# Attention with a soft mixture of experts on one core: contiguous tables and loads, one more weight quarter held early, plain maxima for the last queries

## The chip, the cores and the metric

The kernel runs on one core of one Trainium2 chip. The metric is the device time of one execution in microseconds (us); lower is better. The kernel before has a median of 422.11 us over three runs (420.61 to 422.81).

## What is computed

Causal attention with a cumulative bias over 8 batches of 8 heads (576 positions, 64 channels), then a mixture of experts in which softmax weights over all 4608 tokens mix the tokens into 32 slots, eight two-layer networks work on the slots, and a second softmax spreads the slots back.

```python
scores = scale * q @ k.T                       # per head, 576 x 576
bias   = -(cum[:, None] - cum[None, :])        # cum = cumsum(max(s, 0))
scores = where(causal, -1e9, scores + min(bias, 0))
attn   = exp(scores - scores.max(-1)); attn /= attn.sum(-1) + 1e-9
x      = attn @ v                              # then tokens x 512
logits = x @ phi                               # 32 slots, 4 for each expert
d = softmax over tokens(logits); slot_in = d.T @ x
slot_out[e] = max(slot_in[e] @ w1[e], 0) @ w2[e]
out = softmax over slots(logits) @ slot_out
```

## The kernel before, in words

The work goes by 32 pairs p of heads, four to a batch. A table written out by hand, ORDER, sets the order of every step; each step issues its instructions on its engines as the table comes to it, and each engine then works through its own list in that order. `x.p` below is step x of pair p.

**Scores.** `load` fetches a pair's transposed queries and keys. `cast` (ScalarE) rounds them into a tile `w` and `low` (VectorE) writes the remainders behind, so that three passes of matmuls give nearly full precision. A tile `g` holds in a few rows the cumulated bias and, later, the row maxima, each as a high and a low part; the matmuls of `mx` and `s` take `g` as one more factor. `mx.p.i` (TensorE, L367) computes approximate scores, `red.p.i.a` (VectorE, L379) takes their maxima for head a: a custom instruction adds a mask of 0 and -3e38 and reduces, and each is followed by one that reads its accumulator. Group 0 are keys 0 to 287 of the last 128 queries, group 1 the remaining 288 keys of these queries, started from group 0's maximum. `f0`, `f1`, `f2` split and transpose the maxima, and `md` sends them into `g` (two DMAs); `cum` sends the bias rows (two DMAs).

**Attention.** `s` (L429) computes exact transposed scores less the maxima, `ex` (ScalarE, L440) the exponentials, `cut` (GpSimd, L447) the causal corner, `zc` and `z` the sums over key blocks, `load_v` fetches the values (two DMAs), `ax` and `a` (L511, L522) multiply with them, and `sm` (L551) adds up the denominators of a batch in one bank.

**Normalization.** After a batch's last `sm`, `e1` takes the reciprocals (L631, L632) and `rw` writes them to a table `rs` in DRAM (L636). `rd.p` reads a pair's rows of the table back, spread to 64 partitions per head (L561, two DMAs), `nr.p` (VectorE, L584) multiplies. `nat` transposes for TensorE's next product and `lt` forms the logits. The last two pairs take `rb` (L572), which spreads by matmuls instead of through DRAM.

**The expert stage.** The weights are 64 quarters of 512 KB each. 23 are fetched into `pre` during the attention (`pre.i`), 27 into space that falls free at its end (`get.i`), and the rest by `refill` into quarters that have been used. The weight and output DMAs are all issued by SyncE (SP) in program order. `mlp1` (L983) and `mlp2` (L1011) are the two layers for four experts at a time; `ct`, `cd` and `ct7` transpose the second softmax's weights of batches; `pick` (L1020) selects each slot's own expert out of the products; `two` (L1040) and `heads` spread the slots, evict and send out.

```python
1011  nc.tensor.matmul(ps[32 * g:32 * g + 32, :], ht[eg][:, fc, 32 * g:32 * g + 32], ...)
1014  (nc.scalar.copy if eg else nc.vector.tensor_copy)(sos[half][:, eg, :], ps)
```

SP takes its list in order too: an `rd` that waits for its `rw` to land holds back the loads behind it.

## Time and profile before

| | |
|---|---|
| median of three runs | 422.11 us |
| span of the profiled execution | 419.0 us |
| what lies around the span, at the median | 3.1 us |
| TensorE busy | 397.0 us (95%) |
| VectorE, GpSimd, ScalarE busy | 286.6, 281.4, 240.9 us |
| moved by DMA | 82.72 MB in 54037 packets |

The profiled execution's own time is its span of 419.0 us; no other time of that one execution is among those shown. Busy time counts overlapping instructions of an engine once. TensorE runs at full granted clock until its work ends.

### The profile page before, as it was taken

The numbers are of one execution on the slowest core, as the hardware profiler recorded it, in microseconds if no ns is written. First come the engines' busy times: TensorE is split into PE (matmuls) and PEld (weight loads), VectorE is DVE, ScalarE is ACT, GpSimd is POOL, SyncE is SP. The second block draws the span as 40 slices with busy tenths as digits, with TensorE's granted clock in tenths as the row PEclk, the third lists the DMA queues.
The fourth block names the chain that finished last, engine by engine and source line by source line (L and its number), as shares of the span: only waits on it lengthen the run. The fifth ranks groups of instructions, "written<-read, shape, count | busy, mean of one in ns | idle before, by whom it ended". The sixth has DMA issues, their size and how long they took to land.

```text
span 419.0 us, 14779 instructions
## 1 busy us (share of the span) xinstructions
PE 397.0 (95%) x5703; PEld 296.6 (71%) x5703; DVE 286.6 (68%) x1012; ACT 240.9 (58%) x719; POOL 281.4 (67%) x387
## 2 busy tenths in 40 slices
PE   8999999889999999999999999999999999999960
PEld 8877777776777777777777777778777767435540
DVE  7966787987787788777867877787778446211460
ACT  3166666665657666766686768676855753220450
POOL 8178999877877888898878898887888730000000
PEclk9999999999999999999999999999999999999995
DMA  3424578624774558455754674363227869999998
GB/s 128 144 61 145 169 262 227 184 83 143 188 208 140 173 164 236 119 167 161 209 163 144 175 215 140 92 176 115 89 85 179 256 192 390 407 406 408 324 338 294
DMA packets 54037, 82.72 MB, mean 197 GB/s; under 512 B 5584, under 2 KB 40912, under 8 KB 53968
## 3 DMA queue, kind: packets, MB, share of 16 engines
q1 hardware_dynamic: 53952, 81.78, 62.1%
q8 instruction: 45, 0.74, 0.7%
q14 instruction: 24, 0.20, 0.2%
q10 hardware_dynamic: 16, 0.01, 0.0%
HBM read 71.38 MB, written 10.03 MB: 194 GB/s over the span
## 4 chain that ended last, share of the span: by engine, by line
PE 77%; DVE 5%; DMA 5%; issue 2%; POOL 1%; SPq 1%; ACT 1%; DVEq 0%
PE s L429 23%; PE y L522 18%; PE mx L367 10%; PE sum L551 4%; DMA arena<-rs 3%; PE m L1011 3%; PE nat L592 3%; PE m L983 3%; PE lt L655 2%; DVE arena L584 2%; PE sl L776 1%; PE mt L398 1%; DVE junk L379 1%; PE po L1046 1%; PE x L511 1%
## 5 line engine op out<-in xcount | busy, mean ns | idle before, releaser
L379 DVE CUSTOM_DVE_ANT_0 junk<-mx,arena 128x320 bf16<-128x320 f32 (+3 forms) x320 | 125.7, 427 | 51.9 <-PE mx L367 24.7
L440 ACT ACTIVATE arena<-s 128x288 f32<-128x288 f32 (+4 forms) x384 | 115.0, 408 | 30.5 <-PE s L429 29.4
L429 PE MATMUL s<-w 64*128 64x288 f32 (+4 forms) x1152 | 109.2, 304 | 0.2 <-DVE nmin L733 0.2
L522 PE MATMUL y<-arena 128*64 128x512 f32 (+4 forms) x640 | 91.1, 427 | 0.4 <-POOL arena L447 0.4
L429 PEld LDWEIGHTS s<-w 64*128 64x128 f32 (+1 forms) x1152 | 81.8, 177 | 10.2 <-ACT arena L440 1.1
L447 POOL TENSOR_SCALAR_AFFINE_SELECT arena<-arena 128x256 f32<-128x256 f32 (+1 forms) x160 | 67.6, 437 | 21.3 <-ACT arena L440 19.2
L522 PEld LDWEIGHTS y<-arena 128*64 128x64 f32 x640 | 42.9, 137 | 45.1 <-issue 34.1
L468 POOL TENSOR_TENSOR arena<-arena 128x896 f32<-128x896 f32 x31 | 68.2, 2202 | 7.4 <-PE mt L398 4.6
L367 PE MATMUL mx<-w 64*128 64x288 f32 (+4 forms) x384 | 57.2, 302 | 1.5 <-DVE mx L379 0.8
L429 PE MATMUL s<-g 64*128 64x288 f32 (+4 forms) x384 | 56.3, 290 | 0.0
L367 PE MATMUL mx<-g,ones 64*128 64x288 f32 (+4 forms) x384 | 53.5, 300 | 0.0
L339 DVE TENSOR_TENSOR w<-arena,w 128x576 fp32r<-128x576 f32 x64 | 51.2, 820 | 0.1
L470 POOL TENSOR_TENSOR arena<-arena 128x640 f32<-128x640 f32 x31 | 48.0, 1547 | 2.4
L334 ACT CAST w<-arena 128x576 fp32r<-128x576 f32 x64 | 40.3, 677 | 13.4 <-DMA arena<-in_qk_dram 12.6
L534 ACT COPY arena<-y 128x512 f32<-128x512 f32 x32 | 18.8, 588 | 49.5 <-PE y L522 49.5
L367 PEld LDWEIGHTS mx<-w 64*128 64x128 f32 x384 | 39.0, 185 | 4.1 <-DVE mx L379 1.4
L367 PEld LDWEIGHTS mx<-g,ones 64*128 64x128 f32 x384 | 38.6, 185 | 0.3
L429 PEld LDWEIGHTS s<-g 64*128 64x128 f32 (+1 forms) x384 | 35.0, 177 | 0.5
L472 POOL TENSOR_TENSOR arena<-arena 128x384 f32<-128x384 f32 x31 | 31.9, 1029 | 2.4
L584 DVE TENSOR_TENSOR arena<-arena 128x576 f32<-128x576 f32 x30 | 27.7, 929 | 7.3 <-DMA arena<-rs 5.2
L379 DVE CUSTOM_DVE_ANT_0 junk<-mx,arena,mx 128x288 bf16<-128x288 f32 x64 | 30.7, 516 | 2.5 <-PE mx L367 1.2
L379 DVE DVE_READ_ACCUMULATOR2_ANT mx<- 128x1 f32 (+1 forms) x384 | 31.5, 82 | 0.0
(170 smaller groups left out, 515.2 us busy)
## 6 DMA issues: line engine op xcount, KB each, us to landing
arena<-in_qk_dram SPq DMA_DIRECT2D x32, 576.0 KB
pre<-in_w_dram SPq DMA_DIRECT2D x36, 512.0 KB
arena<-in_w_dram SPq DMA_DIRECT2D x19, 512.0 KB
arena<-rs SPq DMA_DIRECT2D x60, 144.0 KB
arena<-in_v_dram SPq DMA_DIRECT2D x32, 256.0 KB
out_dram<-pre SPq DMA_DIRECT2D x16, 256.0 KB
ww<-in_w_dram SPq DMA_DIRECT2D x6, 512.0 KB
out_dram<-arena SPq DMA_DIRECT2D x10, 256.0 KB
```

Source lines behind the costliest of these rows:

```text
L334: nc.scalar.copy(w[:, QO + S * i:QO + S * (i + 1)], st["raw", p][:, i, :])
L339: nc.vector.tensor_tensor(w[:, QO + S * (2 + i):QO + S * (3 + i)], st["raw", p][:, i, :], w[:, QO + S * i:QO + S * (i + 1)].bitcast(F32), ...
L367: nc.tensor.matmul(ps[a][:, d:d + hi - lo], l[r], t[r, KO + lo:KO + hi], start=t is w, stop=t is gt)
L379: nc.vector.tensor_tensor_reduce(out=junk[r, 0:w], in0=ps[r, d:d + w], in1=mask[r, o:o + w], scale=1.0, scalar=m[:, a, 4:5] if i == 1 else ...
L429: nc.tensor.matmul(ps[a][0:n, d:d + hi - lo], t[r, ko + 128 * j:ko + 128 * j + n], t[r, qo + lo:qo + hi], start=x == 0, stop=x == 3)
L440: nc.scalar.activation(st["p", p][0:n, a, o + lo:o + hi], ps[0:n, d:d + hi - lo], AF.Exp, bias=0.0, scale=0.125)
L447: nc.gpsimd.affine_select(d, d, pattern=[[0, 2], [1, n]], compare_op=ALU.is_ge, fill=0.0, base=0, channel_multiplier=-1)
L468: eng.tensor_tensor(z[:, :, 128:576], pt[:, :, 128:576], pt[:, :, 576:1024], op=ALU.add)
L470: eng.tensor_tensor(z[:, :, 256:576], z[:, :, 256:576], pt[:, :, 1024:1344], op=ALU.add)
L472: eng.tensor_tensor(z[:, :, 384:576], z[:, :, 384:576], pt[:, :, 1344:1536], op=ALU.add)
L522: nc.tensor.matmul(y[r, lo - 64:512], vt[:, j, r], st["p", p][:, g, OFF[j] + lo - 128 * j:OFF[j] + 576 - 128 * j], start=(j == 0), stop=(j ...
L584: nc.vector.tensor_tensor(u, u, st.pop(("r", p)), op=ALU.mult)
```

## The change

The scores and the order of the steps stay as they are; ORDER gains one word, `pre.23`. What is changed:

- **A 24th quarter** of weights is fetched during the attention, so that 13 are left to `refill` and not 14. The room comes from smaller tiles: the mask in 16 bits, `w` without its pad, and one buffer fewer for the discarded output `junk` and for `hl`.
- **Group 0** of the maxima is a plain reduce without mask.
- **Rows of `g`** lie on partitions 0, 32, 64 and 96 (bias) and the partition behind each (maxima), so that `md` (from pair 1) and `cum` (from pair 4) are one DMA each.
- **Values** are laid out on the host as the tile wants them, zeros included: one DMA of 2560 bytes a partition.
- **The table `rs`** holds each head's 576 reciprocals in order: `rw` scatters them with two DMAs, and `rd` reads one run of 2304 bytes for each partition and not two of 1152.
- **At the start** fewer memsets on GpSimd.
- **In the expert stage** the eviction of `mlp2` masks and adds the two groups of experts on VectorE, so that `pick` is one matmul. The transposes for `dn` (`cd`) move behind the first half's output, and `ct7` becomes a `ct` ahead of the output of batches 4 and 5.

```diff
-NPRE = 23
+NPRE = 24
...
-    size = dict(raw=2 * S, p=3200, u=S, v=640, z=2 * S, r=S, x=NCH * DM, mask=S - 128, phi=HP * NS, ls=192)
+    size = dict(raw=2 * S, p=3200, u=S, v=640, z=2 * S, r=S, x=NCH * DM, mask=S // 2 - 64, junk=S // 2 - 64, phi=HP * NS, ls=192)
...
-    mask = reg("mask", 0)
+    mask = reg("mask", 0).bitcast(BF16)
...
-        nc.gpsimd.memset(t[:, 0:KO].bitcast(F32), 0.0)
-        for a in (0, 64):
-            nc.gpsimd.memset(t[a:a + 4, 0:KO].bitcast(F32), 1.0)
+        nc.gpsimd.tensor_copy(t[:, 0:KO], ones2[:, 0:1].bitcast(F32).broadcast_to([128, KO]))
...
+    def every32(t, i):
+        return t.bitcast(F32).rearrange("(a r) x -> a r x", r=32)[:, i, :]
...
+            if p >= HP:
+                nc.sync.dma_start(out=every32(gt, 0)[:, KO:KO + S], in_=cumd[2 * p:2 * p + 2])
+                return
...
+                if i == 0:
+                    nc.vector.tensor_reduce(m[:, a, c:c + 1], ps[:, d:d + w], axis=AX.X, op=ALU.max)
+                    continue
...
+            if p:
+                nc.sync.dma_start(out=every32(gt, 1)[:, 0:KO].rearrange("l (c q) -> l c q", c=NCH), in_=hl.bitcast(F32))
+                return
...
-            nc.sync.dma_start(out=vt[:, 0:4, :],
-                              in_=v[b * S:b * S + 512, 128 * hp:128 * hp + 128]
-                              .rearrange("(j p) c -> p j c", p=128))
-            nc.sync.dma_start(out=vt[0:64, 4, :],
-                              in_=v[b * S + 512:b * S + 576, 128 * hp:128 * hp + 128])
+            nc.sync.dma_start(out=reg("v", p % NV), in_=v[p])
...
-            d = st["rs", b, gi].rearrange("(g f a i) x -> g a f (i x)", g=2, f=2, i=4)
             for g in range(2):
-                nc.sync.dma_start(out=r[64 * g:64 * g + 64].rearrange("p (f x) -> p f x", f=2),
-                                  in_=d[g, hp:hp + 1].broadcast_to([64, 2, S // 2]))
+                nc.sync.dma_start(out=r[64 * g:64 * g + 64], in_=st["rs", b, gi][g, hp:hp + 1].broadcast_to([64, S]))
...
-            d = pd.tile([128, SQ], F32, tag="rs", name=f"rs{b}_{gi}")
-            nc.sync.dma_start(out=d, in_=st["sr", b, gi])
+            d = pd.tile([2, 8, S], F32, tag="rs", name=f"rs{b}_{gi}")
+            for g in range(2):
+                nc.sync.dma_start(out=d[g].rearrange("a (i f x) -> f (a i) x", i=4, f=2),
+                                  in_=st["sr", b, gi][64 * g:64 * g + 64])
...
-        (nc.scalar.copy if eg else nc.vector.tensor_copy)(sos[half][:, eg, :], ps)
+        m = again[left[0]][:, DM + 128 + eg:DM + 129 + eg]
+        if eg == 0:
+            nc.vector.tensor_scalar(sos[half], ps, m, None, op0=ALU.mult)
+        else:
+            nc.vector.scalar_tensor_tensor(sos[half], ps, m, sos[half], op0=ALU.mult, op1=ALU.add)
...
-        for eg in range(2):
-            nc.tensor.matmul(ps[:, 0:HC], sel[eg], sos[half][:, eg, :], start=(eg == 0), stop=(eg == 1))
+        nc.tensor.matmul(ps[:, 0:HC], sel, sos[half], start=True, stop=True)
...
-        if cc == 0:
-            ct7()
...
+        if b == 4:
+            ct(B - 1, B)
...
+    cd(4, B)
```

**SP around batch 1's table.** Rows of SP's list from `rw` of batch 1 to the next weight quarter; `rs` is the table, `sr` the reciprocals, `g` the tile of bias and maxima, `hl` the maxima, `cumd` the bias in DRAM. Before:

```order
L636 DMA rs_0_2010<-sr_0_2002 128x72
L411 DMA g_97<-hl_2025 2x5x128 x2
L349 DMA g_96<-cumd 2x576 x2
L561 DMA arena<-rs_0_2010 64x2x288 x4
L491 DMA arena<-in_v_dram 128x4x128
L494 DMA arena<-in_v_dram 64x128
L850 DMA pre<-in_w_dram 128x1024
```

Now:

```order
L646 DMA rs_0_1905<-sr_0_1898 2x32x72 x2
L424 DMA g_97<-hl_1921 4x5x128
L357 DMA g_96<-cumd 4x576
L571 DMA arena<-rs_0_1905 64x576 x4
L506 DMA arena<-in_v_dram 128x640
L860 DMA pre<-in_w_dram 128x1024
```

Twelve DMAs with one `rw` became ten with two; the transfer of the values is one, and the table's writes lead with a dimension of 2.

**TensorE in `mlp1` of the second group of experts.** `m` are the products, `sit` the slots, `ht` the transposed hidden layer. Before:

```order
L983 MATMUL m_7228<-pre,sit 32x512 x4
L983 MATMUL m_7229<-pre,sit 32x512 x4
L1070 MATMUL ct_7241<-ident,e_nat 128x128
L1071 MATMUL cs_7172<-ident,e_nat 32x64
L983 MATMUL m_7228<-pre,sit 32x512 x4
L983 MATMUL m_7229<-pre,sit 32x512 x4
L1000 MATMUL ht_7254<-ident,ww_6568 128x128 x4
```

Now:

```order
L995 MATMUL m_6905<-pre,sit 32x512 x4
L995 MATMUL m_6906<-pre,sit 32x512 x4
L995 MATMUL m_6905<-pre,sit 32x512 x4
L995 MATMUL m_6906<-pre,sit 32x512 x4
L1012 MATMUL ht_6925<-ident,ww_6254 128x128 x4
L1012 MATMUL ht_6931<-ident,ww_6254 128x128 x4
```

The two transposes of batch 7 have left this place.

**TensorE at `pick` of the first half.** `sel` is the selection, `po` the output's product. Before:

```order
L1011 MATMUL m_7364<-pre,wg_6557 32x256 x2
L1020 MATMUL sel_7369<-pre 128x256 x2
L1011 MATMUL m_7364<-arena,wg_6557 32x256 x2
L1011 MATMUL m_7364<-pre,wg_6557 32x256 x2
L1046 MATMUL po<-pre,e_nat 128x256 x8
```

Now:

```order
L1023 MATMUL m_7035<-pre,arena 32x256
L1035 MATMUL sel_7040<-pre 128x256
L1023 MATMUL m_7035<-arena 32x256 x3
L1023 MATMUL m_7035<-pre,arena 32x256
L1061 MATMUL po<-pre,e_nat 128x256 x8
```

Ahead of the first output one selecting matmul stands where two stood.

## Rows read from the trace of the kernel before

**Rows 1.** The page: span, and busy time of each engine.

```profile
span 419.0 us, 14779 instructions
PE 397.0 (95%) x5703; PEld 296.6 (71%) x5703; DVE 286.6 (68%) x1012; ACT 240.9 (58%) x719; POOL 281.4 (67%) x387
```

**Rows 2.** Stages: length; busy PE, PEld, DVE, ACT, POOL; PE clock, DMA share, GB/s.

```profile
117.40:158.50 41.10, 41.10 (x621) 31.73 (x621) 31.46 (x120) 27.55 (x86) 33.48 (x44) 1.00 0.58 168
76.00:117.40 41.40, 37.42 (x569) 28.98 (x569) 34.52 (x112) 28.01 (x86) 32.86 (x44) 1.00 0.54 158
341.00:388.00 47.00, 46.39 (x623) 25.70 (x623) 16.55 (x41) 11.72 (x33) 1.65 (x5) 1.00 1.01 388
388.00:417.50 29.50, 16.40 (x232) 10.31 (x224) 11.21 (x19) 9.93 (x20) 0.00 (x0) 0.86 0.96 333
```

**Rows 3.** The chain that ended last, near 340 us: start, length, work.

```profile
341.08 6.01 DMA arena<-rs
...
347.18 0.76 DVE arena L584
...
348.77 1.22 PE rb L572 x32
```

**Rows 4.** VectorE's instructions by form, 158.5 to 281.8 us: busy, mean ns, idle before.

```profile
L379 DVE CUSTOM_DVE_ANT_0 junk<-mx,arena 128x288 bf16<-128x288 f32 x24 | 10.1, 446 | 9.9 <-POOL arena L447 9.4 <-PE mx L367 0.5
...
L697 DVE TENSOR_REDUCE mt<-ln 128x5 f32<-128x160 f32 x3 | 1.0, 327 | 0.4
```

**Rows 5.** The end in order of time, TensorE: start, length, instruction, idle before.

```profile
360.32 0.41 PE L940 MATMUL cs<-ident,e_nat 64*32 64x64 f32 x6
...
367.55 1.90 PE L983 MATMUL m<-pre,sit 128*32 128x512 f32 x16
369.38 0.33 PE L1070 MATMUL ct<-ident,e_nat 128*128 128x128 f32 x1
...
369.87 1.92 PE L983 MATMUL m<-pre,sit 128*32 128x512 f32 x16
...
384.82 1.13 PE L1020 MATMUL sel<-pre 128*128 128x256 f32 x4
```

**Rows 6.** The same stretch on ScalarE and SP.

```profile
384.52 0.37 ACT L1014 COPY pre<-m 128x256 f32<-128x256 f32 x1 [7.41 <-PE m L1011]
...
388.41 11.69 SPq L1052 DMA_DIRECT2D out_dram<-pre  x16
```

**Rows 7.** SP's issues around batch 1's table, in order of time.

```profile
104.13 0.33 SPq L636 DMA_DIRECT2D rs<-sr  x1
104.77 1.31 SPq L411 DMA_DIRECT2D g<-hl  x2
...
107.03 1.99 SPq L561 DMA_DIRECT2D arena<-rs  x3
```

**Rows 8.** Who waited for that table: VectorE, then TensorE, then pair 8 in batch 2.

```profile
112.91 0.89 DVE L584 TENSOR_TENSOR arena<-arena 128x576 f32<-128x576 f32 x1 [1.60 <-DMA arena<-rs]
...
117.39 0.66 PE L592 MATMUL nat<-ident,arena 128*128 128x128 f32 x4 [0.62 <-DVE mx L379]
...
153.70 0.76 DVE L584 TENSOR_TENSOR arena<-arena 128x576 f32<-128x576 f32 x1
...
155.74 0.49 PE L592 MATMUL nat<-ident,arena 128*128 128x128 f32 x3
```

**Rows 9.** Three short stretches, columns as in group 2.

```profile
21.50:22.00 0.50, 0.50 (x12) 0.50 (x10) 0.50 (x2) 0.01 (x1) 0.00 (x0) 1.00 0.89 184
106.50:108.50 2.00, 2.00 (x14) 0.77 (x12) 1.94 (x11) 0.67 (x2) 1.84 (x3) 1.00 0.03 9
108.50:109.00 0.50, 0.50 (x8) 0.35 (x6) 0.44 (x4) 0.00 (x0) 0.50 (x1) 1.00 0.85 122
```

**Rows 10.** The last pair's values: TensorE waiting, and SP's first issue of them.

```profile
343.46 0.34 PE L511 MATMUL x<-arena 128*64 128x64 f32 x4 [0.46 <-DMA arena<-in_v_dram]
...
338.65 0.55 SPq L491 DMA_DIRECT2D arena<-in_v_dram  x1
```

More of the change, by code (lines that the diff above doesn't have):

```diff
@@ L160 @@
[L160 to L163 removed]
+a.22.0 cut.23.3 red.25.2.0 z.23.1 a.22.1 red.25.2.1 a.22.2 a.22.3 z.23.2 red.25.1.0 a.22.4 ax.23 red.25.1.1 pre.23
+ev.22 load_v.24 s.24.0 low.26.0 z.23.3 evx.23 s.24.2 low.26.1 ex.24.0.0 f0.25 ex.24.0.1 s.24.1 ex.24.2.0 load.28
@@ L288, in tile_attn_softmoe @@
     nc.gpsimd.memset(reg("x", 0)[64:128, 0:DM], 0.0)
-    for i in range(NV):
-        nc.gpsimd.memset(reg("v", i)[64:128, 512:640], 0.0)
     for i in range(NPB):
@@ L1038, in banks, with part @@
         return [bank("po") for _ in range(n)]
-    def two(b, half):
+    def part(b, n, half):
         c = slice(HC * half, HC * half + HC)
-        po = [x.rearrange("p (b c) -> p b c", b=2) for x in banks(4)]
-        for i in range(2):
+        po = [x[:, 0:HC * n].rearrange("p (b c) -> p b c", b=n) for x in banks(4)]
+        for i in range(n):
             for x, r in zip(po, rows):
@@ L1065, in heads @@
                 nc.sync.dma_start(out=outb[b:b + 2, 0:64].rearrange("i t c -> t i c"), in_=ot[:, x, :])
-    def ct7():
-        pa = bank("ct2")
-        nc.tensor.transpose(pa[:, 0:128], et[:, B - 1, 0:128], ident)
-        nc.tensor.matmul(st["cs", 1][rows[3], 1:128:2], et[0:64, B - 1, 128:160], ident[0:64, 0:64], start=True, stop=True)
-        nc.scalar.copy(et[:, B - 1, 0:128], pa[:, 0:128])
-        cd(1, slice(64, 128))
     late_banks = False
     so = again[left[0]][:, 0:DM]
-    sel = [again[left[0]][:, DM + 128 * eg:DM + 128 * eg + 128] for eg in range(2)]
-    ct(1, 4, B - 1)
+    sel = again[left[0]][:, DM:DM + 128]
+    ct(4, B - 1)
     m = mlp1(0)
@@ L1095, in tile_attn_softmoe @@
     stage = [again[i] for i in left[late:]] + [w2q[e, i] for i in range(2) for e in range(NE)]
-    sos = [again[left[1]][:, DM * half:DM * half + DM].rearrange("p (e c) -> p e c", e=2) for half in range(2)]
+    sos = [again[left[1]][:, HC * half:HC * half + HC] for half in range(2)]
     m = chain(mlp2(0, 0), mlp2(0, 1))
@@ L1105, in tile_attn_softmoe @@
     for b in range(0, B, 2):
+        if b == 4:
+            ct(B - 1, B)
         if b == B - 2:
             steps(m)
-        two(b, 0)
+        part(b, 2, 0)
         steps(m, 4)
@@ L1111, in tile_attn_softmoe @@
     late_banks = True
-    two(0, 1)
+    cd(4, B)
+    part(0, 2, 1)
     heads()
     for b in range(2, B, 2):
-        two(b, 1)
+        part(b, 2, 1)
 def constants():
```

175 lines of the change are left out of this document (92 added, 83 removed).

## The prediction

> **What bounds the kernel now.** I read the page first: TensorE is busy for 397.0 of 419.0 us [rows 1]. The stages say where it isn't. From 117.4 to 158.5 us it is busy for all of 41.10 us while VectorE works 31.46, GpSimd 33.48 and the DMA engines 0.58 of the time [rows 2]; the chain of waits there is TensorE's alone up to some 341 us. A shorter instruction on another engine buys nothing in that stretch. Three places are left. Between 76 and 117.4 us TensorE stands still for 41.40 - 37.42 = 3.98 us [rows 2]. Around 341 to 349 us the chain leaves TensorE for the read of the last batch's table, 6.01 us, then VectorE, then `rb` [rows 3]. From there TensorE's list sets when the first output leaves, at 388.41 us [rows 6], and up to then DMA is full as well, share 1.01 at 388 GB/s; behind it the outputs keep DMA at 0.96 and 333 GB/s to the end [rows 2]. A microsecond off the end counts only if the weights and TensorE's list both become shorter before 388.41.
>
> The sum is made against the profiled execution, span 419.0 us; the median of the runs shown is 3.1 us more, and I add that.
>
> **Part by part.**
>
> *The end, 360 to 388 us.* Six `cs` instructions ahead of `mlp1` go; they last 0.41 us [rows 5], and with the overlap of what follows on TensorE I take 0.34. `ct7` goes from the middle: a step of 16 products starts at 367.55 and the next at 369.87, 2.32 us later; the step's own 1.90 leaves 0.42, and from `ct`'s start at 369.38 to 369.87 are 0.49 [rows 5]. I take 0.50, since a step that is followed by its like overlaps it. `pick`'s four instructions last 1.13 [rows 5], so half of them 0.56; against that the first of the old two started without the second group's eviction, 384.82 beside a copy that ends at 384.52 + 0.37 = 384.89 [rows 5, 6]. Now the one must wait for an eviction on VectorE, some 0.25 later, which leaves 0.30. Together 0.34 + 0.50 + 0.30 = 1.14, say 1.15 us. The cover: one quarter of 512 KB less in the queue is 0.524 MB / 388 GB/s = 1.35 us [rows 2], a little more than 1.15, so the weights are out of the way as early as the first output comes. The 24th quarter moves into a stretch where DMA is idle for four tenths of the time, at nothing. The moved `ct` and `cd` fall between 388 and 400 us, where DMA bounds; nothing, or up to 0.4 if they hold up an output. **Term: -1.15**, between 0 (outputs start no earlier) and -1.35.
>
> *The table `rs`, 66 to 117 us.* Batch 1: `rw` is issued at 104.13, the reads begin at 107.03 [rows 7], VectorE waits 1.60 us for them until 112.91, and TensorE later 0.62 for the maxima queued behind that multiplication [rows 8]. What is new has no row. A read of one head was 128 pieces of 1152 bytes and is 64 of 2304. In the half microsecond in which such reads move, 122 GB/s at share 0.85 [rows 9] is 9.0 GB/s for an engine, 128 ns a piece, 1.02 us a transfer over 16 engines; pieces of 512 bytes beside it run at 184 GB/s and 0.89, 40 ns each. If a read's piece keeps its 9.0 GB/s, 2304 bytes cost 256 ns and nothing is gained; if it costs what it did, 128 ns, half: 0.51 us on each of the four transfers of `rd.4` and `rd.5`, 2.0 us. I take the middle, 1.0. SP issues one `md` where two took 1.31 [rows 7], but a second `rw`, 0.33. The writes keep their 288-byte pieces, 8 an engine if 16 engines serve them as now: no cost beyond the second issue. So the table's readers come about 1.0 us earlier, in batch 0 as in batch 1, and of the 3.98 us of standstill I give back a quarter. **Term: -1.0**, between -4.0 (no standstill left) and +2.0 (the rivals). Batches 2 to 6 have nothing to gain: pair 8's multiplication runs at 153.70 to 154.46 and its transposes at 155.74, 1.28 us of slack [rows 8].
>
> *How many engines write the table.* While only transfers that lead with a dimension of 2 are on their way (`md`, `cum`), DMA's share is 0.03 at 9 GB/s [rows 9], half an engine of 16: such transfers are not spread. The Trainium skill, "DMA: Bandwidth & Descriptors", section "Why a DMA increments its semaphore by 16 and not by 1", says that a transfer uses the largest number of engines up to 16 that divides the outermost sizes of both sides, the lowest-numbered ones. By that the new `rw`, which leads with 2, runs on two engines, both halves on the same two; the trace agrees for `md` and `cum`, and no row shows it for a table. The time by it is the first rival's.
>
> *The last pair, 338 to 349 us.* `load_v.31` begins at 338.65 and TensorE waits 0.46 us for it at 343.46 [rows 10]. One DMA in larger pieces, issued without its second half, takes that wait away; the next to be late is `rd.28`, whose landing at about 347.1 holds `rb` at 348.77 [rows 3] and which moves up behind it. **Term: -0.35**, between -0.6 and +1.5 (the table late).
>
> *The rest, at nothing.* Plain maxima: the masked form of 288 keys takes 446 ns, a reduce of 160 elements out of PSUM 327 [rows 4]; at 1 ns more for each of 128 elements it is 455, and the accumulator's read lay beside the next instruction. 64 instructions by -0.08 to +0.05 us are -5 to +3 us of VectorE time, but VectorE idles 9.6 of 41.1 us [rows 2]: covered, and if that cover fails it is in the range of the second term. The mask in 16 bits changes no element count. The memsets on GpSimd lie before the three places named, and I give their shortening nothing. `md` and `cum` as one DMA each save SP issues, and SP's waits are for data.
>
> **Sum:** -1.15 - 1.0 - 0.35 = -2.5. Span 416.5; with 3.1 around it **419.6 us**.
>
> **The rivals.**
>
> *Two engines write the table, at the cheaper price.* 64 pieces an engine instead of 8, at 40 ns: 2.56 - 0.32, the table lands 2.2 us later, the reads give 1.0 back. Batch 1's standstill grows by some 1.2, batch 0 stays (in SP's list a load of values stands ahead of its first read), batches 2 to 6 use up their 1.28 us of slack, the last pair loses 0.6 and its 0.35. Sum -1.15 + 1.2 + 0.6 = +0.65: **422.8 us**, no change. For: the small share of narrow transfers. Against: eight pieces and their latency took under 2.9 us in all [rows 7], so a piece may cost less. Chance 0.24.
>
> *The same at a dearer price; slower.* At 72 ns, the middle in ratio between 40 and 128, the table lands 4.0 us late, 3.0 after the faster reads. SP stands at the first read of each batch, with loads and `md` behind it; TensorE loses 3.0 - 1.28 = 1.7 in each of five batches, 3.0 in batch 1, 1.5 in batch 0 and 2.0 at the last pair: 15.0 - 1.15 = +13.9, **436 us**. It decides once batches 2 to 6 lose too, from a lateness of about 2.5 us, that is from 44 ns a piece. Against: write pieces elsewhere run at 40. Chance 0.12.
>
> *All standstill goes.* The table lands before VectorE asks, and the maxima behind are never late: -4.0 - 1.15 - 0.6, **416.4 us**. For: 1.60 of waiting starts a chain of lateness. Against: VectorE's own multiplications stretched there too, which nothing here mends. Chance 0.15.
>
> *The end does not move*, because outputs queue behind weights or the moved transposes hold them up, and the rest gives 0.5: **421.6 us**. Chance 0.09.
>
> **How the numbers follow.** The forecast has 0.40; its own range is 418.0 to 421.0. Faster or slower by over 0.5%, about what a measurement can tell from no change here, means under 420.0 or over 424.2. Faster: 0.30 of the forecast's 0.40, 0.15 from the third rival, 0.03 from the first: 0.48. Slower: 0.12 of the second and 0.03 of the first's upper part: 0.15. Same: 0.37. The range leaves out the second rival and the lower edge of the third: 415.9 to 424.3.
>
> **What would show it.** Right: first output at about 385 us of the span, TensorE's idle between 76 and 117 us near 3 us, no wait for values at the last pair, no gap between steps at `ct7`'s old place. Wrong: over 4 us between `rw`'s issue and the first read, waits of VectorE for the table in batches 2 to 6, or TensorE idle in a stage that has none now.

## The result, and the profile after

The changed kernel takes 415.56 us (median of 4 runs, 414.87 to 416.38) where the kernel before takes 422.18 (4 runs, 420.61 to 422.81): a ratio of 0.985, 95% interval 0.981 to 0.989, so 6.6 us or 1.6% faster. The forecast was 419.6; the measured time lies 0.3 us below its range. It is closest to the rival "all standstill goes" (416.4), in number only: that rival gave the whole gain of its stretch to a table that lands earlier, and the runs below show another cause.

The page of the changed kernel, to be held against [rows 1]:

```profile
span 413.9 us, 14533 instructions
PE 395.3 (96%) x5699; PEld 295.3 (71%) x5699; DVE 284.0 (69%) x952; ACT 239.6 (58%) x717; POOL 274.8 (66%) x376
```

TensorE works 1.7 us less and the span is 5.1 us shorter, so most of the gain is standstill that is gone. The stretch for which the forecast's largest term was written, and the one that follows it, columns as in [rows 2]:

```profile
76.00:117.40 41.40, 40.76 (x606) 31.23 (x606) 33.26 (x120) 28.89 (x87) 35.70 (x47) 1.00 0.58 182
117.40:158.50 41.10, 40.91 (x620) 31.26 (x616) 31.64 (x113) 28.04 (x86) 34.35 (x45) 1.00 0.56 174
```

Between 76 and 117.4 us TensorE stands still for 0.64 us, against 3.98 before [rows 2]. A stretch fixed in time does not hold the same work in both kernels, so I set a marker into each pair of heads: the 32 products that sum its probabilities, which stand once per pair in TensorE's list. Their starts in both timelines:

| marker | before, us | after, us | ahead by | gained since the marker above |
|---|---|---|---|---|
| sum of pair 5 | 77.50 | 77.32 | 0.18 | |
| pair 6 | 91.57 | 89.97 | 1.60 | 1.42 |
| pair 7 | 102.45 | 99.64 | 2.81 | 1.21 |
| pair 9 | 125.14 | 120.95 | 4.19 | 1.38 |
| pair 12 | 154.98 | 150.77 | 4.21 | 0.02 |
| pair 13 | 166.23 | 162.49 | 3.74 | -0.47 |
| pair 17 | 207.31 | 204.15 | 3.16 | -0.58 |
| pair 30 | 340.00 | 336.82 | 3.18 | 0.02 |
| pair 31 | 346.78 | 342.92 | 3.86 | 0.68 |
| first output on SP | 388.41 | 383.09 | 5.32 | 1.46 |
| end of the span | 419.0 | 413.9 | 5.1 | -0.2 |

Five gains, then, and two small losses: gains of 1.2 to 1.4 us three times between 77 and 125 us, 0.68 at the last pair, 1.46 at the end. The first two gains are where the table has no part; the third lies in batch 1, behind a late table. This is what the kernel before shows at the three places, first on VectorE and then on GpSimd (start, length, instruction):

```profile
81.19 2.71 DVE L584 TENSOR_TENSOR arena<-arena 128x576 f32<-128x576 f32 x1
...
92.50 2.71 DVE L339 TENSOR_TENSOR w<-arena,w 128x576 fp32r<-128x576 f32 x1
...
114.47 2.17 DVE L584 TENSOR_TENSOR arena<-arena 128x576 f32<-128x576 f32 x1
```

```profile
81.17 2.12 POOL L468 TENSOR_TENSOR arena<-arena 128x896 f32<-128x896 f32 x1
...
92.49 2.11 POOL L468 TENSOR_TENSOR arena<-arena 128x896 f32<-128x896 f32 x1
...
113.92 2.11 POOL L468 TENSOR_TENSOR arena<-arena 128x896 f32<-128x896 f32 x1
```

and TensorE, which waits for the maxima queued behind the first two of those instructions:

```profile
84.65 0.42 PE L655 MATMUL lt<-arena 128*32 128x128 f32 x8 [1.30 <-DVE mx L379]
...
95.96 0.40 PE L367 MATMUL mx<-w 64*128 64x288 f32 x1 [0.82 <-DVE mx L379]
```

The same two places in the changed kernel, VectorE and GpSimd (L593, L347 and L484 are the old L584, L339 and L468):

```profile
80.23 0.82 DVE L389 TENSOR_REDUCE mx<-mx 128x1 f32<-128x288 f32 x2 [0.60 <-PE mx L378]
80.97 0.75 DVE L593 TENSOR_TENSOR arena<-arena 128x576 f32<-128x576 f32 x1
...
90.83 0.75 DVE L347 TENSOR_TENSOR w<-arena,w 128x576 fp32r<-128x576 f32 x1
```

```profile
81.00 2.70 POOL L484 TENSOR_TENSOR arena<-arena 128x896 f32<-128x896 f32 x1
...
90.89 2.65 POOL L484 TENSOR_TENSOR arena<-arena 128x896 f32<-128x896 f32 x1 [0.16 <-PE mt L411]
```

Read the starts. At the first two places of the kernel before, VectorE's instruction of 576 columns begins 0.02 and 0.01 us behind GpSimd's addition and lasts 2.71 us in place of 0.75: it ends 0.61 us behind the addition, as it does at the third place, where it began 0.55 us late. In the changed kernel it begins 0.03 and 0.06 us ahead and lasts 0.75, and now the addition is the longer one, 2.7 in place of 2.1. Both read two operands from SBUF. The Trainium skill, "SBUF — State Buffer", section "Who interferes with whom", says that a VectorE instruction with two SBUF inputs and a GpSimd instruction that reads SBUF share a path which the first to issue holds for its whole instruction; these rows agree, 2.71 against 0.75. Below, such an overlap is a meeting, and the engine that is held up has lost it.

The forecast's own three places, in the changed kernel. SP around batch 1's table and at the first output:

```profile
101.32 1.14 SPq L646 DMA_DIRECT2D rs<-sr  x2
102.55 0.58 SPq L424 DMA_DIRECT2D g<-hl  x1
103.23 0.53 SPq L357 DMA_DIRECT2D g<-cumd  x1
103.85 2.41 SPq L571 DMA_DIRECT2D arena<-rs  x4
...
383.09 15.54 SPq L1067 DMA_DIRECT2D out_dram<-pre  x20
```

The first read leaves 2.53 us behind the write's issue, against 2.90 [rows 7], and SP's waits for such writes shrank from 2.8 to 0.7 us over the whole kernel: the rival that made the kernel slower by a late write did not come about. The write itself did go to fewer engines, by all that the trace shows to two. The records of its 128 pieces of 288 bytes name no engine, but they run two at a time, first one half and then the other, from 102.51 to 103.72 us, and while the second half moves the DMA share is 2.2 engines of 16:

```profile
103.16:103.72 0.56, 0.56 (x10) 0.43 (x8) 0.56 (x5) 0.56 (x3) 0.41 (x1) 1.00 0.14 33
```

But a piece lasts 19 ns in the records and the next starts 15 ns after it, so the write needs 1.1 to 1.2 us from first piece to last in each of the eight batches; in batch 1 of the kernel before it needs 0.84. The reads: while almost nothing but table pieces moves, of 1152 bytes before and of 2304 now, the rows are

```profile
108.50:111.50 3.00, 3.00 (x48) 2.65 (x45) 2.74 (x10) 1.52 (x6) 2.40 (x4) 1.00 0.74 148
```

```profile
104.50:107.00 2.50, 2.50 (x28) 1.50 (x26) 2.37 (x11) 0.38 (x1) 2.28 (x3) 1.00 0.42 146
105.50:106.00 0.50, 0.50 (x8) 0.25 (x6) 0.47 (x3) 0.00 (x0) 0.50 (x1) 1.00 0.52 184
```

148 GB/s at share 0.74 are 12.5 GB/s for an engine, 92 ns a piece of 1152 bytes; 146 at 0.42 are 22, 106 ns a piece of 2304. Over the whole kernel the records of such pieces have means of 80 and 121 ns. The half microsecond of [rows 9], 128 ns a piece, is the start of a burst and dearer than the rest. By these means a read of one head needs 0.48 us of 16 engines in place of 0.64, so it gained 0.16 us and not 0.5.

The two losses have one cause, from the chain of waits:

```profile
152.00 6.41 DMA g<-hl
...
193.54 6.54 DMA g<-hl
```

The shifts `md` need 6.4 and 6.5 us from issue to their first use, and TensorE's products stand for them.

### The profile page after: what moved, and what is told of

Its sections match the earlier page's. It is cut to its first block, busy times and chain, and to the rows that moved or that the text cites. A ratio compares the mean times of both kernels' runs of the same rounds, so it can differ in the third digit from the quotient of the medians.

```text
span 413.9 us, 14533 instructions
## 1 busy us (share of the span) xinstructions
PE 395.3 (96%) x5699; PEld 295.3 (71%) x5699; DVE 284.0 (69%) x952; ACT 239.6 (58%) x717; POOL 274.8 (66%) x376
## 4 chain that ended last, share of the span: by engine, by line
PE 81%; DMA 4%; DVE 3%; ACT 2%; issue 2%; SPq 0%; DVEq 0%
PE s L445 25%; PE y L533 19%; PE mx L378 11%; PE sum L562 4%; PE m L1023 3%; PE m L995 3%; DMA g<-hl 3%; PE nat L601 3%; PE lt L666 2%; PE sl L786 2%; PE mt L411 1%; PE po L1061 1%; ACT arena L456 1%; PE x L522 1%; DVE arena L392 1%
## 5 line engine op out<-in xcount | busy, mean ns | idle before, releaser
L463 POOL TENSOR_SCALAR_AFFINE_SELECT arena<-arena 128x256 f32<-128x256 f32 (+1 forms) x160 | 63.7, 411 | 23.6 <-ACT arena L456 22.0
L484 POOL TENSOR_TENSOR arena<-arena 128x896 f32<-128x896 f32 x31 | 69.3, 2237 | 8.7 <-PE mt L411 5.9
L392 DVE CUSTOM_DVE_ANT_0 arena<-mx,arena 128x448 bf16<-128x448 f32 (+3 forms) x128 | 59.0, 461 | 17.6 <-PE mx L378 15.8
L392 DVE CUSTOM_DVE_ANT_0 junk<-mx,arena 64x64 bf16<-64x64 f32 (+3 forms) x128 | 49.2, 385 | 10.4 <-PE mx L378 8.7
L347 DVE TENSOR_TENSOR w<-arena,w 128x576 fp32r<-128x576 f32 x64 | 50.6, 810 | 0.2
L389 DVE TENSOR_REDUCE mx<-mx 128x1 f32<-128x288 f32 x64 | 26.7, 447 | 27.5 <-PE mx L378 23.3
L403 POOL TENSOR_SCALAR mh<-mx 128x10 fp32r<-128x10 f32 x32 | 20.1, 627 | 17.5 <-DVE mx L392 17.1
```

The lines of the kernel that those rows point to most:

```text
L347: nc.vector.tensor_tensor(w[:, o + 2 * S:o + 3 * S], st["raw", p][:, i, :], w[:, o:o + S].bitcast(F32), op=ALU.subtract)
L389: nc.vector.tensor_reduce(m[:, a, c:c + 1], ps[:, d:d + w], axis=AX.X, op=ALU.max)
L392: nc.vector.tensor_tensor_reduce(out=junk()[r, 0:w], in0=ps[r, d:d + w], in1=mask[r, o:o + w], scale=1.0, scalar=m[:, a, 4:5] if i == 1 el ...
L463: nc.gpsimd.affine_select(d, d, pattern=[[0, 2], [1, n]], compare_op=ALU.is_ge, fill=0.0, base=0, channel_multiplier=-1)
L484: eng.tensor_tensor(z[:, :, 128:576], pt[:, :, 128:576], pt[:, :, 576:1024], op=ALU.add)
```

## The experiments

The first question was what took the three waits between 77 and 125 us away. **Theory A**: the order in which VectorE's instruction and GpSimd's addition start; the plain maxima and the faster transfers both only shift that order. **Theory B**, the forecast's: the table. Later C and D on which transfers matter. "Before" and "changed" name the two kernels; each kernel is one of them with one edit. Medians are of 4 to 10 runs, ratios against runs of the kernel before beside them.

### One part alone, one part undone

**b_plain**, before with plain maxima alone:

```diff
+                if i == 0:
+                    nc.vector.tensor_reduce(m[:, a, c:c + 1], ps[:, d:d + w], axis=AX.X, op=ALU.max)
+                    continue
```

> The kernel before with one edit: the maxima over the 288 keys of group 0 as plain maxima. Theory A (start order of VectorE and GpSimd): in the kernel before, two multiplications or subtractions of VectorE started 0.01 to 0.02 us behind GpSimd's 2.1 us addition of 128x896 (81.19 behind 81.17, 92.50 behind 92.49) and took 2.71 us instead of 0.75, and TensorE then waited 1.30 and 0.82 us; in the changed kernel VectorE starts 0.03 and 0.06 us ahead of it (80.97 against 81.00, 90.83 against 90.89) and takes 0.75, while GpSimd takes 2.7. Two plain maxima in a row end some 0.02 to 0.04 us earlier than two masked ones, so this edit alone should win both starts: TensorE's standstill between 76 and 117.4 us falls from 3.98 to about 1.5, the time by 2 to 3 us to about 419.7. Theory B (the table, as forecast): nothing waits for these maxima that the table has not made late, so the standstill stays near 4 us and the time within 0.5 us of 422.2.

Measured: 420.89 us, ratio 0.996 (0.993 to 0.999). Both waits of batch 0 are gone, as A said. VectorE, then GpSimd:

```profile
80.64 0.75 DVE L587 TENSOR_TENSOR arena<-arena 128x576 f32<-128x576 f32 x1
...
90.50 0.75 DVE L339 TENSOR_TENSOR w<-arena,w 128x576 fp32r<-128x576 f32 x1
...
110.78 2.44 DVE L587 TENSOR_TENSOR arena<-arena 128x576 f32<-128x576 f32 x1 [0.42 <-DMA arena<-rs]
```

```profile
80.66 2.71 POOL L471 TENSOR_TENSOR arena<-arena 128x896 f32<-128x896 f32 x1
...
90.56 2.66 POOL L471 TENSOR_TENSOR arena<-arena 128x896 f32<-128x896 f32 x1 [0.15 <-PE mt L401]
...
110.49 2.12 POOL L471 TENSOR_TENSOR arena<-arena 128x896 f32<-128x896 f32 x1
```

But the time fell by 1.7 us only. This profile, of the fastest of its ten runs, shows three waits of TensorE, 1.05 us each at 113.97, 156.15 and 280.50; the first stands for the 0.53 and 0.62 us of the kernel before, the other two are new. The last row of each fence shows where they come from: in batch 1 the multiplication by the divisors waits 0.42 us for the table's read, so begins 0.29 us behind the addition and pays for it. The table matters here, but through the same meeting.

**b_table**, before with the table alone (the columns of `sm` and `rb` follow it as in the change):

```diff
-            d = pd.tile([128, SQ], F32, tag="rs", name=f"rs{b}_{gi}")
-            nc.sync.dma_start(out=d, in_=st["sr", b, gi])
+            d = pd.tile([2, 8, S], F32, tag="rs", name=f"rs{b}_{gi}")
+            for g in range(2):
+                nc.sync.dma_start(out=d[g].rearrange("a (i f x) -> f (a i) x", i=4, f=2),
+                                  in_=st["sr", b, gi][64 * g:64 * g + 64])
...
+                nc.sync.dma_start(out=r[64 * g:64 * g + 64], in_=st["rs", b, gi][g, hp:hp + 1].broadcast_to([64, S]))
```

> The kernel before with one edit: the table of divisors as 2 x 8 x 576, written by two transfers and read in pieces of 2304 bytes. Theory A: only the waits of batch 1's table go (0.53 and 0.62 us of TensorE at 113.94 and 117.39) and part of the last pair's, 1.1 to 1.9 us, to about 420.8; the two standstills at 84.65 and 95.96 stay at 1.30 and 0.82. Theory B: all 3.98 us of standstill between 76 and 117.4 us go, to about 418.2. Theory C (the writes on few engines make the table late): slower than 422.2.

Measured: 422.40 us, ratio 1.0005 (0.997 to 1.004): nothing. The wait of 1.30 us in batch 0 stays (at 84.94); the one of 0.82, which A let stay too, is gone, since VectorE starts level with the addition there and wins. The multiplication comes second in batches 1, 2 and 3, with waits of 0.99 to 1.34 us behind it. B has fallen.

**a_masked**, the changed kernel with masked maxima again:

```diff
-                if i == 0:
-                    nc.vector.tensor_reduce(m[:, a, c:c + 1], ps[:, d:d + w], axis=AX.X, op=ALU.max)
-                    continue
```

> The changed kernel with one part undone: group 0's maxima masked again. Theory A: VectorE's next instruction falls behind GpSimd's addition again at one or both places, takes about 2.7 us there, and TensorE stands still 1 to 2.6 us more between 76 and 117.4 us: 416.5 to 418.5. Theory B: no change, 415.6 within 0.5.

Measured: 418.09 us, ratio 0.990 (0.987 to 0.993), 2.5 us more than the changed kernel. Both waits are back in their old sizes:

```profile
85.20 0.43 PE L663 MATMUL lt<-arena 128*32 128x128 f32 x8 [1.30 <-DVE mx L389]
...
96.54 0.40 PE L378 MATMUL mx<-w 64*128 64x288 f32 x1 [0.84 <-DVE mx L389]
```

**a_table**, the changed kernel with the old table, b_table's edit the other way round:

```diff
-            d = pd.tile([2, 8, S], F32, tag="rs", name=f"rs{b}_{gi}")
...
+            d = pd.tile([128, SQ], F32, tag="rs", name=f"rs{b}_{gi}")
+            nc.sync.dma_start(out=d, in_=st["sr", b, gi])
```

> The changed kernel with one part undone: the table as 128 x 72, one write, reads in pieces of 1152 bytes. Theory A: VectorE waits for batch 1's table again and TensorE loses 1.1 to 1.4 us there, and up to 0.7 at the last pair: 416.7 to 417.7. Theory B: 4 us come back between 76 and 117.4 us, 419.5 or more.

Measured: 416.50 us (414.3 to 417.9), ratio 0.985 (0.979 to 0.992), and no wait for divisors that reaches TensorE in its profile. Less than A allowed, nothing of B's 4 us, and with four runs not to be told from the changed kernel.

### Moving a start

**b_poolwait**, before with a memset of 128x1 ahead of each addition:

```diff
             if i == 0:
+                if p < NP - 1:
+                    nc.gpsimd.memset(idle, 0.0)
```

> The kernel before with work added: one memset of 128 x 1 on GpSimd ahead of each of its 31 additions of 128x896, nothing else. Theory A (whoever starts first holds the other up): GpSimd's addition now starts a tenth of a microsecond or more later, VectorE's 576-wide instruction starts ahead of it at 81.2 and 92.5 us and takes about 0.75 us instead of 2.71, and TensorE's waits of 1.30 and 0.82 us go: 420 to 421 in the median though work was added, and the profile without those two waits. Theory B (the two long instructions of VectorE have another cause): both waits stay and the time is 422.5 or, by the memsets, more.

Measured: 421.03 us, ratio 0.998 (0.995 to 1.001), both waits still there. The edit was no delay: the addition began 0.02 and 0.01 us ahead of VectorE's instruction as before, since the memset lay in the tail of the instruction ahead of it. Nothing follows from it.

**a_dvewait**, changed, with a memset of 128x1 on VectorE behind the second plain maximum:

```diff
+                    if a == 1:
+                        nc.vector.memset(idle, 0.0)
                     continue
```

> The changed kernel with one memset of 128 x 1 on VectorE behind the second plain maximum of each pair, 32 in all, each expected to last under 0.1 us. Theory A: VectorE's next instruction falls behind GpSimd's addition at 81.00 and 90.89 us (margins 0.03 and 0.06 us), takes about 2.7 us, and TensorE waits 1.3 and 0.8 us more: the time grows by 2 us or somewhat less, to 417 to 418. Theory B: 32 instructions of 0.06 us beside idle VectorE: no change, 415.6 within 0.5.

Measured: 415.71 us, ratio 0.982 (0.979 to 0.986). The 0.06 us lay inside the next instruction's record; again no delay and no verdict.

**a_twice**, changed, the second maximum taken twice:

```diff
-                    nc.vector.tensor_reduce(m[:, a, c:c + 1], ps[:, d:d + w], axis=AX.X, op=ALU.max)
+                    for _ in range(1 + a):
+                        nc.vector.tensor_reduce(m[:, a, c:c + 1], ps[:, d:d + w], axis=AX.X, op=ALU.max)
```

> The changed kernel with the second plain maximum of each pair taken twice (the same value once more), 32 instructions of 0.39 us. Theory A: VectorE's next instruction starts some 0.35 us behind GpSimd's addition in place of 0.03 to 0.06 ahead, takes 2 us or more, and TensorE waits again in batch 0, 1 to 2.1 us in all: 416.6 to 418. Theory B: VectorE, idle for a fifth of the time, absorbs 0.39 us for each pair: 415.6 within 0.5.

Measured: 426.50 us, ratio 1.010 (1.005 to 1.016): 10.9 us more than the changed kernel for 12.5 us of work on an engine that idles a fifth of the time. VectorE now comes second at every meeting, and TensorE waits in every batch:

```profile
86.83 0.43 PE L667 MATMUL lt<-arena 128*32 128x128 f32 x8 [1.31 <-DVE mx L393]
...
98.16 0.40 PE L378 MATMUL mx<-w 64*128 64x288 f32 x1 [0.83 <-DVE mx L393]
...
119.44 0.66 PE L602 MATMUL nat<-ident,arena 128*128 128x128 f32 x4 [1.05 <-DVE mx L393]
...
161.74 0.66 PE L602 MATMUL nat<-ident,arena 128*128 128x128 f32 x4 [1.05 <-DVE mx L393]
```

The same wait, 1.05 us (1.04 once), stands in each of batches 1 to 6. My expectation had batch 0 only, so it was too small; its direction is A's.

**b_poolwait2**, as b_poolwait with a longer memset:

```diff
-    idle = top.tile([128, 1], F32, name="idle")
+    idle = top.tile([128, 320], F32, name="idle")
```

> The kernel before with a longer memset on GpSimd, 128 x 320, ahead of each of its 31 additions of 128x896. The memset of one element was no delay at all: GpSimd's addition still started 0.02 us ahead of VectorE's instruction (81.46 against 81.48, 92.79 against 92.80). This one should last some 0.3 us. Theory A (whoever starts first holds the other up for its whole instruction): VectorE now starts first, takes 0.75 us, TensorE's waits of 1.3 and 0.8 us at about 85 and 96 us go, and the time falls by 2 us, to 420.2, though work was added. Theory B (another cause, in VectorE itself): both waits stay, 422 or more.

Measured: ratio 1.014 (1.007 to 1.020), some 6 us slower. VectorE won the second place (0.75 us) but lost the first with a start recorded 0.18 us ahead (3.27 us), and later ones at 0.11 and 0.16 ahead. With a long instruction right before the addition, being ahead of the addition isn't enough. As a test of A it decides nothing.

**b_split** and **a_split**, the addition in two halves:

```diff
-                eng.tensor_tensor(z[:, :, 128:576], pt[:, :, 128:576], pt[:, :, 576:1024], op=ALU.add)
+                for a in range(2):
+                    eng.tensor_tensor(z[:, a, 128:576], pt[:, a, 128:576], pt[:, a, 576:1024], op=ALU.add)
```

> The kernel before with GpSimd's addition of 128x896 as two of 128x448, some 1.1 us each. Theory A: VectorE, when it starts second, waits for one half instead of the whole, about 1.8 us in place of 2.71 at both places of batch 0, and TensorE's waits there shrink from 1.30 and 0.82 us to 0.3 and 0; likewise the 1.05 us in later batches: 419.5 to 420.7. Rival: GpSimd keeps the path over both halves, since its next instruction is waiting: no change, 422.2, or somewhat more by 31 further instructions.

> The changed kernel with the same split. Theory A: it has one such loss left (2.00 us for 0.75 at 70 us, with waits of 0.33 and 0.30 behind it): a gain of 0 to 0.6 us in the median and a smaller spread, 414.9 to 415.6. Rival as above: 415.6 or up to 0.5 more.

Measured: b_split ratio 1.013 (1.004 to 1.021); a_split 427.06 us, ratio 1.012 (1.009 to 1.015), 11.5 us more than the changed kernel. VectorE and GpSimd in a_split, batch 2:

```profile
155.76 3.32 DVE L594 TENSOR_TENSOR arena<-arena 128x576 f32<-128x576 f32 x1
```

```profile
155.86 2.24 POOL L485 TENSOR_TENSOR arena<-arena 128x448 f32<-128x448 f32 x2
```

VectorE waits for both halves, 3.32 = 0.75 + 2.24 + 0.3, and it does so although its record begins 0.10 us earlier. The rival was right that GpSimd keeps the path from one half to the next, though it forecast at most 0.5 us for it; and the recorded starts are not the moment at which the path is granted.

**b_wait**, the kernel before with the order fixed by a semaphore: GpSimd first copies one column of the result of VectorE's latest 576-wide instruction.

```diff
             if i == 0:
+                if p < NP - 1:
+                    nc.gpsimd.tensor_copy(idle, st["wide"])
                 eng.tensor_tensor(z[:, :, 128:576], pt[:, :, 128:576], pt[:, :, 576:1024], op=ALU.add)
```

(`st["wide"]` is set to that column behind `low` and behind the multiplication in `nr`.)

> The kernel before with one thing added: ahead of each of the 31 additions of 128x896 GpSimd copies one column of the result of VectorE's latest 576-wide instruction, so it cannot start the addition before that instruction is done. Masked maxima, old transfers and old end stay. Theory A (the order alone costs the waits): no 576-wide instruction beside an addition over 1 us, the waits of 1.30 and 0.82 us in batch 0 and of 1.05 us in later batches gone, the time down by 2 to 4 us to 418.2 to 420.2. Rival (GpSimd has no time to wait): its later start holds up the sums of the probabilities and the copies that share its list, 422.2 or more.

Measured: 417.97 us, ratio 0.990 (0.986 to 0.995), 4.0 us less than the kernel before, with its masked maxima, its transfers and its end all in place. VectorE and GpSimd:

```profile
81.12 0.76 DVE L588 TENSOR_TENSOR arena<-arena 128x576 f32<-128x576 f32 x1
...
91.06 0.75 DVE L340 TENSOR_TENSOR w<-arena,w 128x576 fp32r<-128x576 f32 x1
```

```profile
81.94 0.18 POOL L471 COPY idle<-arena 128x1 f32<-128x1 f32 x1 [0.92 <-DVE arena L588]
82.08 2.12 POOL L472 TENSOR_TENSOR arena<-arena 128x896 f32<-128x896 f32 x1
...
92.02 2.11 POOL L472 TENSOR_TENSOR arena<-arena 128x896 f32<-128x896 f32 x1
```

The addition starts some 0.9 us later (82.08 against 81.17) and TensorE waits for nothing there. One 576-wide instruction of over 1 us is left beside an addition, 1.59 us at 70 us. This settles theory A: the meeting alone costs the kernel before about 4 us (2.2 to 6.1 by the interval). With the 0.9 us of the end below that is 5 of the 6.6; no run places the rest, which is within the intervals.

**a_wait**, the same in the changed kernel:

```diff
+                if p < NP - 1:
+                    nc.gpsimd.tensor_copy(idle, st["wide"])
```

> The changed kernel with the same wait. Theory A: VectorE already comes first in eight of nine meetings, so only the one at 70 us is left (2.00 us, 0.63 us of TensorE's waiting behind it): 415.0 to 415.6. Rival: the addition starts up to 0.6 us later in all 31 pairs and something behind it is late: 415.6 to 417.

Measured: 416.27 us (414.8 to 417.4), ratio 0.988 (0.984 to 0.994); not below the changed kernel. Its meetings were already won; what the wait adds cannot be told from nothing.

### Which transfers

Theory C: values, shifts and sums crowd the queue ahead of the divisors' reads. D: they don't matter.

**a_v2**, changed with the values by two transfers in pieces of 512 bytes; **b_v1**, before with the values by one, shown here (a_v2 is its reverse; the host's layout goes with it, and in a_v2 memsets of the zeros):

```diff
-            nc.sync.dma_start(out=vt[:, 0:4, :],
...
-            nc.sync.dma_start(out=vt[0:64, 4, :],
...
+            nc.sync.dma_start(out=reg("v", p % NV), in_=v[p])
```

> The changed kernel with one part undone: the values by two transfers in pieces of 512 bytes. In the runs so far those with the old lists of transfers show waits of about 1.05 us of TensorE for maxima behind a multiplication that was late for its divisors (three in one with plain maxima alone, three in one with the new table alone), and those with the changed lists almost none, with the old table too. Theory C (the values' small pieces and second issue hold up the divisors' reads on the queue and the DMA engines): one to three such waits come back, 416.6 to 418.6. Theory D (it is the shifts and sums, md and cum, or the table): 415.6 within 0.5.

> The kernel before with one edit: the values of a pair by one transfer of 128x640 from a host layout that fits. Theory C: the divisors land earlier, the 1.05 us waits in batches 1 to 7 go, and VectorE's wait of 1.6 us in batch 1 shrinks; the two waits of batch 0 stay: 419.5 to 421. Theory D: 422.2 within 0.7. The forecast gave this part 0.35 us, at the last pair.

Measured: a_v2 417.27 us, ratio 0.988 (0.983 to 0.993), with no wait for divisors in its profile but one of 1.09 us for the bias rows at 60.84; b_v1 423.29 us, ratio 1.001 (0.997 to 1.005), with three waits of 1.05. Alone the values do nothing. Nor does one transfer take TensorE's wait for the last pair's values away, in b_v1's profile:

```profile
346.25 0.34 PE L506 MATMUL x<-arena 128*64 128x64 f32 x4 [0.73 <-DMA arena<-in_v_dram]
```

**a_md2**, changed with the shifts by two transfers for each pair:

```diff
-            if p:
-                nc.sync.dma_start(out=every32(gt, 1)[:, 0:KO].rearrange("l (c q) -> l c q", c=NCH), in_=hl.bitcast(F32))
-                return
```

> The changed kernel with one part undone: the shifts of the scores (md) come by two transfers of 2x5x128 for each pair, as before, instead of one of 4x5x128. In the profile of the changed kernel TensorE waits for this transfer at 158.46 and 200.13 us (0.19 and 0.32 us there; its products come 1.05 us later in all), 6.4 us from issue to landing. If one transfer that leads with 4 is slower than two that lead with 2, those waits go and the time falls by up to 1 us, to 414.6 to 415.6; if the landing is late because of what is queued ahead on the DMA engines, the waits stay, 415.6 or, by one more issue of SP for each pair, up to 0.5 more.

Measured: 416.54 us (414.4 to 417.1), ratio 0.984 (0.979 to 0.988). The waits for the shifts are not in its profile, one wait of 1.04 us for divisors is. They are not in a_table's or a_end's profile either, where the shifts come by one transfer, so the two losses of the table above can't be laid to the one transfer alone. Of the 11 profiles with one transfer four show TensorE waiting for the shifts, 0.2 to 0.8 us in all, of the nine with two transfers none: that speaks for the one transfer and is too little to show it.

**b_three**, before with all transfers changed (the edits of b_table and b_v1, the rows of `g` 32 apart, `md` and `cum` by one transfer each, with the fill of `g` at the start that goes with the rows):

```diff
+                nc.sync.dma_start(out=every32(gt, 0)[:, KO:KO + S], in_=cumd[2 * p:2 * p + 2])
...
+                nc.sync.dma_start(out=every32(gt, 1)[:, 0:KO].rearrange("l (c q) -> l c q", c=NCH), in_=hl.bitcast(F32))
```

> The kernel before with all of its transfers changed (the shifts and sums by one transfer each, the values by one, the table in its new form) and nothing else. Theory C (each shortens the same queue, and only together do they bring the divisors in before VectorE asks): VectorE's multiplication starts 0.16 us ahead of GpSimd's addition in all of batches 1 to 6, no wait of 1.05 us there; batch 0's two waits (1.30 and 0.82 us) stay: 419.4 to 420.4. Theory D (the transfers do nothing and the rest of the gain lies in the end): 422.2 within 0.7.

Measured: 418.17 us, ratio 0.989 (0.983 to 0.995): 4.3 us less, more than C expected. In its profile VectorE starts 0.16 us ahead in all of batches 1 to 6 and no wait of 1.05 us is left; at 93 us it wins too, and the wait of 1.31 us at 85.17 stays.

### The end

**a_q23**, changed with 23 quarters (and `pre.23` out of the order), and **a_end**, changed with the old expert stage:

```diff
-NPRE = 24
+NPRE = 23
```

```diff
+        if cc == 0:
+            ct7()
...
-        nc.tensor.matmul(ps[:, 0:HC], sel, sos[half], start=True, stop=True)
+        for eg in range(2):
+            nc.tensor.matmul(ps[:, 0:HC], sel[eg], sos[half][:, eg, :], start=(eg == 0), stop=(eg == 1))
```

> The changed kernel with one part undone: 23 quarters of the weights fetched early instead of 24. The forecast's cover: 0.524 MB at 388 GB/s, 1.35 us of DMA, comes back ahead of the first output; if the weights set when it leaves, the first output moves from 383.1 to 384.4 us and the time grows by about 1.3 us to 416.9; if TensorE's list sets it, no change, 415.6 within 0.5.

> The changed kernel with the expert stage of the kernel before (the order of the transposes, two products for each selection, plain evictions). The forecast gave this part 1.15 us. If TensorE's list sets the first output: 41.3 us from the last sum to the first output instead of 40.17, the time 1.1 to 1.5 us longer, 416.7 to 417.1. If DMA sets it: no change, 415.6 within 0.5.

Measured: 416.47 us (414.9 to 417.3), ratio 0.985 (0.981 to 0.989), and 415.83 us (415.6 to 417.0), ratio 0.983 (0.977 to 0.989). Neither median can be told from 415.56. The profiles say more: from the last sum to the first output are 40.17 us in the changed kernel and, within 0.01, in a_q23, a_table, a_masked, a_v2 and a_wait (40.32 in a_md2, 40.72 in a_dvewait); 41.22 in a_end, b_table, b_three, b_v1 and b_wait (41.32 in b_plain, 41.91 in b_poolwait, 41.63 in the profile of before). The new end is worth 1.05 us there, and 0.9 at the end of the span (71.85 against 70.98 from the last sum); the other 0.4 of the 1.46 in the table of markers belongs to the profiled execution of before. The 24th quarter moves the first output by nothing.

### The meetings in one table

The start of VectorE's 576-wide instruction against the start of GpSimd's addition, and its length, from the timelines of the two engines:

| kernel | at 81 to 83 us | at 91 to 95 us | lost in batches 1 to 6 |
|---|---|---|---|
| before | +0.02, 2.71 | +0.01, 2.71 | 1 of 6 (+0.55, 2.17) |
| b_plain | -0.02, 0.75 | -0.06, 0.75 | 3 (+0.14 to +0.29) |
| b_table | +0.03, 2.71 | 0.00, 0.75 | 3 (+0.18 to +0.38) |
| b_v1 | +0.03, 2.71 | 0.00, 0.76 | 3 (+0.10 to +0.61) |
| b_three | +0.03, 2.71 | 0.00, 0.75 | 0 (-0.16 or -0.17) |
| a_masked | +0.03, 2.71 | +0.01, 2.73 | 0 (-0.16) |
| changed | -0.03, 0.75 | -0.06, 0.75 | 0 (-0.21) |
| a_twice | +0.46, 2.28 | +0.44, 2.31 | 6 (+0.27 to +0.29) |

Of the others, a_table, a_v2, a_q23, a_end and a_dvewait win as the changed kernel does; a_md2 loses one in batch 2 (+0.49, 2.25), b_poolwait both of batch 0 and one in batch 1 (+0.16, 2.93).

Plain maxima move VectorE's start from +0.02 to -0.03; divisors that land in time keep it at -0.16 or -0.21 in place of up to +0.61. Both parts of the change buy the same thing, the plain maxima mostly in batch 0 and the transfers behind it: alone 1.7 and 4.3 us, with about 1 for the end 7.0, where the whole change brings 6.6. a_end, which has both without the new end, is 6.7 below the kernel before (4.9 to 9.6 by its interval). The 25 runs of the kernel before beside b_plain lie between 420.3 and 426.1 us. That fits: each meeting lost costs TensorE about 1 us, and which are lost differs between profiles. Run by run it is not shown.

## Why the prediction was wrong

- **The end, -1.15: right by the profiles, not told by the medians.** 1.05 measured; its parts, a_end against the changed kernel, are 0.25, 0.62 and 0.18 where I had 0.34, 0.50 and 0.30. Its cover was not needed: the first output comes as early with 23 quarters, so TensorE's list sets it and not the weights.
- **The table, -1.0: the step that failed.** Of 3.98 us of standstill I gave "back a quarter"; 3.3 went. I had followed the chain from VectorE's wait of 1.60 us in batch 1 [rows 8] and laid all standstill of the stretch to the table. Over half of it (1.42 + 1.21 of the 4.0 us gained there) lay in batch 0, where VectorE waited for no table at 81 and 92 us. The cause was the order of two starts on VectorE and GpSimd: fixed alone (b_wait) it gave 4.0 us, and the table by itself (b_table) nothing. "Batches 2 to 6 have nothing to gain" came from one execution; b_plain, b_table and b_v1 lose meetings there, about 1 us each.
- **Plain maxima at nothing: wrong in the same place.** I priced 64 instructions by their length and found them covered by VectorE's idle time. The price was right, 446 ns measured for an estimate of 455 and for 446 with the mask; what counted was the start of the next instruction, 0.05 us earlier against its rival. The sentence that should have stopped me is in the third rival: "VectorE's own multiplications stretched there too, which nothing here mends". I saw the stretched rows, did not ask what stood beside them on GpSimd, and so took for fixed what hung on 0.02 us.
- **Two engines for the table: right on the engines, as far as the trace tells, wrong on the price.** The write ran two pieces at a time, but at 15 ns from piece to piece and not 40 or 72, so the first read came 2.53 us behind it. The 40 ns were a misreading: in the stretch 21.50 to 22.00 of [rows 9] the 20 packets that move are loads of 4608 bytes; pieces of 512 take 28 ns. The share of 0.03 was no sign of narrow transfers either, since in those 2 us only 20 pieces of data moved. **The reads**: a piece of twice the bytes cost half as much again (80 to 121 ns), not the same.
- **The last pair, -0.35**: the marker shows 0.68, but the kernels with old transfers b_plain, b_poolwait and b_wait have 6.10 or 6.11 us between the last two sums, as the changed kernel has, and the profile of before 6.78. That wait belonged to that one execution, and with one transfer of the values b_v1 still has it, 0.73 us.
- **The addition around the span: 3.1 us, wrong.** In the runs that show both, 1.9 to 2.0 us lie around the span of the kernel before and 1.7 around that of the changed one. So the profiled execution of before took, as an estimate, about 421.0, 1.2 us less than its median, and a sum made against it misses that part: the 6.6 us of the medians are 5.1 of the spans, 0.2 to 0.3 around them, and that 1.2.
- **Not foreseen:** about 1.05 us lost to the shifts in batches 3 and 4.

What stays open: when exactly the path between VectorE and GpSimd is granted (a_split and b_poolwait2 lost with earlier recorded starts), why `md` took 6.4 us twice, and which of the four transfers bring the divisors in early: the table and the values, made or undone alone, and `md` undone changed nothing clear; `md` and `cum` were not made alone in the kernel before, and `cum` was not undone.

## What to carry to other kernels

Where an instruction is three times as long as its like, look at what stands beside it on the other engines in that very microsecond before giving its wait to the nearest late transfer: here VectorE and GpSimd met at one path, and 0.02 us decided 2. If such a meeting costs, fix its order with a semaphore (4.0 us here) rather than with a shorter or longer instruction; and distrust a part that is "covered" by idle time when it moves the start of something that meets another engine.

## What the runs showed of the hardware

- GpSimd keeps the path over instructions that stand behind one another: two halves of 1.12 us held VectorE for 3.32 us, where one of 2.12 held it for 2.71.
- VectorE's masked maxima, one operand in PSUM and one in SBUF, are not held: 320 and 192 columns took 0.48 and 0.35 us inside GpSimd's addition of 128x640, and 0.49 and 0.35 with no addition beside them.
- An instruction of one column is no delay: 0.06 us on VectorE and 0.09 on GpSimd moved no start against the other engine by more than 0.02 us.
- Table reads: pieces of 1152 bytes took 80 ns on average in the kernel before, pieces of 2304 took 121 in the changed one; in stretches of such reads 12.5 and 22 GB/s for an engine.
- A table write that leads with 2 ran two pieces at a time: 64 pieces of 288 bytes in 0.56 us at a DMA share of 0.14, each 19 ns long and 15 ns behind the one before it.
